# One product for v and U of a head in a chunked RWKV-7 plus SiLU kernel, with a planner that judges by four cases

## The chip, the cores and the metric

The kernel runs on one NeuronCore of a Trainium2 chip. Its engines work side by side from queues of their own: TensorE (PE; its weight loads are listed apart as PEld), VectorE (DVE), ScalarE (ACT), GpSimd (POOL) and SyncE (SP), which here only issues DMAs. The metric is the device time of one execution in microseconds (us), lower is better. The clock of TensorE is granted in steps; the profile gives the share of full speed.

## The reference

The first part is a recurrence over 768 tokens for 4 batches and 8 heads of width 40. The second feeds its output, 3072 tokens of 320 channels, through a feed-forward layer of width 2048.

```python
for t in range(S):
    kt, vt, rt = (k[:, :, t], v[:, :, t], r[:, :, t])
    wt, at, bt = (w[:, :, t], a[:, :, t], b[:, :, t])
    y[:, :, t] = np.einsum('bhd,bhde->bhe', rt, state)
    Sa = np.einsum('bhde,bhe->bhd', state, at)
    state_decay = state * wt[:, :, None, :] - np.einsum('bhd,bhe->bhde', Sa, bt)
    state = state_decay + np.einsum('bhd,bhe->bhde', vt, kt)
...
h = x @ w_in
g = h * (1.0 / (1.0 + np.exp(-h)))
return (g @ w_out)
```

Everything is float32.

## The kernel before

**Steps.** The tokens are cut into 12 steps of C = 64. Within a step the recurrence is written as products of 64 x 64 and 64 x 40 blocks for each of the 32 pairs of batch and head. A step n has these parts, each a function that adds operations to a plan:

- `load` and `load_r` bring a, b, k, w, r and v by DMAs on SP's queue; `prepare` makes decayed copies with scans on DVE and the block products on PE (line 682);
- `special` (steps 0 to 2) and `inverse` with `merge` (later steps) give the inverse X of a triangular block;
- `chain` makes R, then U = -(X R) in two layouts. `solve` (line 1135) gives it by token for the state's update (line 1223). `solve_t` (line 1166) gives it by channel, and the copy `turned` takes it on ACT from PSUM to SBUF (a helper records it as line 407);
- `read` makes the output. In `look` (line 1269) r is multiplied with v and with U, all by channel. DVE masks the result (line 1281) into `lam`; `write` (line 1323) multiplies that with kt, DVE scales it (line 1334), and the result goes by DMA through DRAM to `xt`;
- `moe` is the feed-forward part: `full` (line 1405), `rest` (line 1418), SiLU on ACT (line 1428), `second` (line 1445), a copy on DVE and the output's DMA. Its products are added to the plan for every step and fill PE between the small products of the other parts.

In the first steps `weights` also turns the float64 weights into float32 on DVE and ACT, with some sums on PE (line 508).

**The look products.** Partitions 0 to 39 hold the channels of heads of one group (b = 0), partitions 64 to 103 those of the other. `vut` is a tile of [128, 2, 16, 64]: index 1 is the role, v in half 0 and U in half 1. For each m (half of the heads) `look` issues 32 products: 16 heads, each with v and with U. The weights are 40 partitions by 64 columns of `vut`, the moving operand is 64 columns of r. The result of v goes to the half b of the PSUM partitions, that of U to the other half, in the bank b. In the profile a float32 product is two pairs of a weight load (LDWEIGHTS) and a product (MATMUL), so that a look shows 64 pairs.

v arrives in `vut` by four DMAs a step, each of 48 partitions by 2 x 256 floats. `turned` copies all 128 partitions of the PSUM tile in one instruction (in step 0, halves m go one by one).

**The order.** Nothing is ordered by hand. `Plan.order` simulates the engines: each operation has a cost, keys that it reads and writes, PSUM rooms and a priority, and the next on each engine is the one that can start soonest, with priority as a weighted bonus. On PE it adds a change of shape (`turn`, with LEAVE and ENTER) and the fetch of instructions in blocks of 256 (`walk`). `best` draws 10 settings of the weights and then takes 400 steps of a random search with a fixed seed. Each order found is timed by `through` under several CASES (fetch times, DMA rate, hop between engines, slowness of DVE), and the order with the smallest sum is issued. So a changed cost, key, shape or case can change the order of every engine's instructions.

Of the kernel before, what the change touches and what calls it, by code (L numbers as in the profile page):

```python
# [11 lines left out]
F32 = mybir.dt.float32  # L12
# [21 lines left out]
class Plan:  # L34
# [32 lines left out]
    RATE, LAND = 300.0, 2.0  # L67
    COLD = 42.0
    URGE = {"SP": 0.0, "ACT": 0.03, "PE": 0.05, "DVE": 0.1, "POOL": 0.02}
    LEAVE = {"F": 0.09, "R": 0.2, "T": 0.13, "Q": 0.13, "H": 0.12, "S": 0.11}  # L70
    ENTER = {"F": 0.08, "R": 0.1, "T": 0.03, "Q": 0.03, "H": 0.03, "S": 0.03}

    def turn(self, op):

# [102 lines left out]
    def through(self, out, crowd, rate, hop, slower):  # L177
# [6 lines left out]
        fetched, count, shape, work = [0.0, 0.0], 0, "Q", {}  # L184
        before, after = self.SLOW
        width, few = self.WINDOW, self.FEW
        for op in out:
            e = op["engine"]
            s = at[e]
            for b in op["before"]:  # L190
                s = max(s, end[b] + (hop if self.ops[b]["engine"] != e else 0.0))
            for place in op["takes"]:
                s = max(s, free.get(place, 0.0))
            if e == "PE":
                self.shape = shape
                t, shape = s + self.turn(op), op["shape"]
                to_ = count + op["k"]
                step = op["cost"] / op["k"]
                while count < to_:
                    block = count // 256  # L200
                    gate = 256 * block + 194
                    if len(fetched) == block + 1:
                        full = crowd if max(queue.values()) > t + 1 else 0.0
                        fetched.append(max(t + 0.4, fetched[-1] + before) + after + full)
                    if count >= gate:
                        t = max(t, fetched[-1] + 0.1)
                    to = min(to_, gate if count < gate else 256 * block + 256)
                    left, count = (to - count) * step, to
                    while left > 1e-9:
# [79 lines left out]
def kernel(  # L289
# [15 lines left out]
    nc = tc.nc  # L305
# [5 lines left out]
    T = B * C  # L311
# [65 lines left out]
    def act(n):  # L377
        return 0.19 + n * 0.00082
# [11 lines left out]
    def half(i):  # L390
        return slice(64 * i, 64 * i + 64)
# [193 lines left out]
    def load_r(n):  # L585
        pri = 10 * n - 4
        late = [[("@", ("in", "X", 0))], [("@", ("xt", 0, 0))]][n] if n < 2 else []
        for b in range(2):
            for j in range(2):
                src = most(j)  # L590
                dma(
                    lambda b=b, j=j, src=src: nc.sync.dma_start(
                        rs[most(b), 8 * j : 8 * j + 8].rearrange("p (m q) t -> p m (q t)", m=2), channel(rT, n)[b, src]
                    ),
                    80,
                    late,
                    [("r", b, j)],
                    pri,
                )
                dma(  # L600
                    lambda b=b, j=j, src=src: nc.sync.dma_start(
                        vut[most(b), 0, 8 * j : 8 * j + 8].rearrange("p (m q) t -> p m (q t)", m=2), channel(vT, n)[b, src]
                    ),
                    80,
                    late,
                    [("vt", b, j)],
                    pri,
                )

    def prepare(n):  # L610
        pri = 10 * (n - 2) + 6 if n != 1 else -8
# [480 lines left out]
    def chain(n):  # L1092
# [78 lines left out]
                        stop=True,  # L1171
                    )

        def turned(part, pw):
            c = slice(256 * part[0], 256 * part[-1] + 256)
            copy(
                "ACT",
                vut[:, 1].rearrange("p (g x) t -> p x g t", x=2)[:, :, 4 * part[0] : 4 * part[-1] + 4],
                pw.tile[:, :, c].rearrange("p x (g t) -> p x g t", t=C),
                -1.0,  # L1180
            )

        for part in halves(n):
            l = len(part)
            p_ = pri + 0.2 if n else pri - 0.5
            xp = [k for k in xkeys if k[0] != "X2" or k[2] in part]
            pw = pw_[part]
            add("PE", 0.46 * l, partial(solve_t, part, pw), [*xp, ("R", i3)], [pw, *[("ut", m) for m in part]], p_, [pw], 64 * l)
# [58 lines left out]
    def read(n):  # L1247
# [3 lines left out]
        Z = wz[i3][:, 0 : Q * C]  # L1251
        allw = [("wz", i3)]
        ktk = [("kt", i3, 0), ("kt", i3, 1)]
        rk, vtk = [("r", b, j) for b in range(2) for j in range(2)], [("vt", b, j) for b in range(2) for j in range(2)]
        lam, lks = [], []
        for m in range(2):
            pl, la, lk = Room("pair", 2), Room("lam", 3), []
            lam.append(la)
            if n == 0:
                la.tile, lk = ((at[0], [("a", 0)]), (sbs[0], [("sb", 0)]))[m]  # L1260
                lks += lk
            lr = [la] if n else []

            def look(m=m, pl=pl):
                for o in problems("j", "z", "x", "role", "b"):
                    b, j, x, z, role = (o[k] for k in ("b", "j", "x", "z", "role"))
                    hh, c = 8 * j + 4 * m + 2 * z + x, 4 * j + 2 * z + x
                    hu = 8 * m + 4 * j + 2 * z + x if role else hh
                    nc.tensor.matmul(  # L1269
                        pl.tile[half(1 - b if role else b), b, c * C : c * C + C],  # L1270
                        lhsT=vut[rows(b), role, hu, :],
                        rhs=rs[rows(b), hh, :],
                        start=True,
                        stop=True,
                    )
# [384 lines left out]
```

## Time and profile before

| | |
|---|---|
| median of 3 runs | 736.9 us (732.19, 736.9, 741.88) |
| the profiled execution | 742.53 us, span 740.8 us, 27,279 instructions |
| mean granted clock of PE | 0.976 |
| DVE busy | 419.5 us (57%) |
| ACT busy | 194.6 us (26%) |
| DMA | 77.15 MB, 117,979 packets, mean 104 GB/s |
| half-clock stretches of PE after 40 us, by the clock record | 53.2 to 66.9, 77.1 to 80.5, 200.0 to 203.4, 247.8 to 251.2, 565.2 to 572.0 us, and the end |
| first feed-forward product (line 1405) | 77.24 us |
| U copies on ACT (line 407, vut) | 13, of 1.02 us each (0.60 us for the two halves of step 0) |
| look products (line 1269) | 1,536 pairs, from 58.9 to 666.0 us |

The profile is one execution. A row of instructions gives line, engine, operation, tiles out<-in, shapes, count, busy time and mean length of one, then the idle time of the engine just before them with what ended it. Products overlap in PE's pipeline: the mean of 228 ns for a look product is a latency, and the rate is read from the timeline, where 128 pairs of looks pass in about 2 us.

### The profile page before, as it was taken

What the parts mean: (1) busy time and instruction counts of PE and PEld (TensorE: products, weight loads), DVE (VectorE), ACT (ScalarE), POOL (GpSimd) and SP (SyncE); (2) the same over time, 40 slices, a digit from 0 to 9 for tenths busy, and PEclk for the clock granted to TensorE, in tenths of its full rate; (3) what the DMA queues carried; (4) which work ended last, traced back from release to release, by engine and by line L of the source; (5) the groups of instructions that cost most, each with busy time, mean ns of one, the idle gap of its engine ahead of it and who ended that gap; (6) DMA issues with size and microseconds to landing.
All of it is one profiled execution on the core that took longest, in us unless ns stands there. A gap on an engine that the chain in (4) does not pass through costs nothing.

```text
span 740.8 us, 27279 instructions
## 1 busy us (share of the span) xinstructions
PE 674.7 (91%) x12666; PEld 540.5 (73%) x12666; DVE 419.5 (57%) x614; ACT 194.6 (26%) x241; POOL 14.3 (2%) x31
## 2 busy tenths in 40 slices
PE   2179799898899999999999999899999999999995
PEld 2176577678678677878778878778777778788773
DVE  6845799976479256299273397362686449321000
ACT  3251635523212411404304205124114211202020
POOL 2300000000000000000000000000000000000000
PEclk9996999999999999999999999999998999999998
DMA  7770654742632453525353506333233321401000
GB/s 248 160 227 11 195 210 126 222 116 47 161 107 58 96 135 98 139 61 125 112 133 106 161 19 144 95 99 92 73 93 81 97 60 32 126 21 41 18 1 22
DMA packets 117979, 77.15 MB, mean 104 GB/s; under 512 B 65506, under 2 KB 114338, under 8 KB 117218
## 3 DMA queue, kind: packets, MB, share of 16 engines
q1 hardware_dynamic: 113352, 64.54, 32.9%
q0 software_dynamic: 2096, 10.49, 4.3%
q8 instruction: 101, 1.65, 0.9%
q10 hardware_dynamic: 2410, 0.30, 0.3%
q14 instruction: 20, 0.16, 0.1%
HBM read 60.29 MB, written 14.61 MB: 101 GB/s over the span
## 4 chain that ended last, share of the span: by engine, by line
PE 80%; DVE 8%; DMA 3%; ACT 3%; issue 3%; SPq 1%; ACTq 1%; DVEq 0%
PE pair L1445 27%; PE pair L1405 21%; PE pair L1418 5%; PE pair L1269 4%; PE pair L682 3%; PE pair L1323 3%; PE pair L958 2%; PE pair L1135 2%; PE pair L1223 2%; PE pair L1068 1%; PE pair L1166 1%; PE pair L508 1%; PE pair L744 1%; PE pair L1308 1%; PE pair L1111 1%
## 5 line engine op out<-in xcount | busy, mean ns | idle before, releaser
L1445 PE MATMUL pair<-wo,gts 128*128 128x320 f32 x768 | 219.8, 442 | 1.1 <-issue 1.1
L1445 PEld LDWEIGHTS pair<-wo,gts 128*128 128x128 f32 x768 | 144.7, 192 | 60.4 <-issue 4.3
L1405 PE MATMUL pair<-xt,wi 128*128 128x256 f32 x768 | 175.5, 386 | 1.6 <-ACT R L756 1.3
L1405 PEld LDWEIGHTS pair<-xt,wi 128*128 128x128 f32 x768 | 145.7, 192 | 24.5 <-ACT R L756 1.4
L1428 ACT ACTIVATE gts<-pair 128x1024 f32<-128x1024 f32 x48 | 46.5, 1020 | 134.5 <-PE pair L1418 108.3
L682 PE MATMUL pair<-a,kb 40*64 40x64 f32 x1536 | 32.2, 236 | 35.8 <-DVE a L654 28.7
L1457 DVE COPY ot<-pair 128x320 f32<-128x320 f32 x24 | 11.8, 490 | 92.4 <-PE pair L1445 88.9
L796 DVE TENSOR_REDUCE XI<-XI 128x64 f32<-128x512 f32 (+9 forms) x85 | 58.6, 690 | 2.9
L682 PEld LDWEIGHTS pair<-a,kb 40*64 40x64 f32 x1536 | 28.6, 149 | 38.5 <-issue 20.5
L1418 PE MATMUL pair<-xt,wi 64*128 64x256 f32 x384 | 47.9, 389 | 0.0
L1281 DVE TENSOR_TENSOR lam<-pair,ml 128x1024 f32<-128x1024 f32 x22 | 26.4, 1220 | 32.9 <-PE pair L1269 30.4
L1418 PEld LDWEIGHTS pair<-xt,wi 64*128 64x128 f32 x384 | 35.1, 187 | 6.7 <-issue 2.6
L795 DVE TENSOR_TENSOR XI<-XI,mi 128x1024 f32<-128x1024 f32 (+8 forms) x60 | 33.6, 559 | 9.6 <-DMA mi<-md 8.3
L1334 DVE TENSOR_TENSOR lam<-pair,wz 128x1024 f32<-128x1024 f32 x11 | 13.5, 1223 | 38.8 <-PE pair L1323 38.8
L1269 PEld LDWEIGHTS pair<-r,vut 40*64 40x64 f32 x1536 | 25.9, 142 | 6.8 <-issue 5.9
L664 DVE TENSOR_TENSOR kb<-kbv 128x512 f32<-128x512 f32 (+1 forms) x36 | 29.7, 861 | 0.3
L1269 PE MATMUL pair<-r,vut 40*64 40x64 f32 x1536 | 28.5, 228 | 1.2 <-issue 1.2
L627 DVE TENSOR_TENSOR_SCAN kbv<-wz,zt 128x1024 f32<-128x1024 f32 x12 | 27.5, 2291 | 0.5
L645 DVE TENSOR_TENSOR_SCAN wz<-wz,zt 128x1024 f32<-128x1024 f32 x12 | 27.5, 2289 | 0.3
L756 ACT COPY R<-pair 128x640 f32<-128x640 f32 x12 | 8.3, 693 | 67.1 <-PE pair L744 61.5
L795 DVE TENSOR_TENSOR XI<-XI,xs 128x1024 f32<-128x1024 f32 (+1 forms) x25 | 25.3, 1010 | 0.8
L407 ACT ACTIVATE vu<-pair 64x640 f32<-64x640 f32 x13 | 9.1, 698 | 60.3 <-PE pair L1135 59.4
(151 smaller groups left out, 687.7 us busy)
## 6 DMA issues: line engine op xcount, KB each, us to landing
wz<-in_wT SPq DMA_DIRECT2D x12, 512.0 KB
kbv<-in_bT SPq DMA_DIRECT2D x12, 512.0 KB
a<-in_aT SPq DMA_DIRECT2D x12, 512.0 KB
kbv<-in_kT SPq DMA_DIRECT2D x12, 512.0 KB
r<-in_rT SPq DMA_DIRECT2D x48, 96.0 KB
vut<-in_vT SPq DMA_DIRECT2D x48, 96.0 KB
vu<-in_v SPq DMA_DIRECT2D x24, 160.0 KB
out<-ot SPq DMA_DIRECT2D x48, 80.0 KB
```

The costliest lines, as they stand in the source:

```text
L627: nc.vector.tensor_tensor_scan(back(V), back(W[:, 2 : 2 + Q * C]), zt, 1.0, ALU.mult, ALU.add)
L645: nc.vector.tensor_tensor_scan(Z, Z, zt, 0.0, ALU.mult, ALU.add)
L664: TTn[engine].tensor_tensor(out=at_(kb, place(is_b, first), (576 * step, 4 // step), (128, 4), (1, C)), in0=blocks((kf, bf)[is_b]), in1=bl ...
L682: nc.tensor.matmul(room.tile[half(b), j, g * C : g * C + C], lhsT=kb[rows(j), place(is_b, q) : place(is_b, q) + C], rhs=A[rows(j), q * C : ...
L795: nc.vector.tensor_tensor(out=at_(tmp, 0, *dims), in0=x, in1=y, op=ALU.mult)
L796: nc.vector.tensor_reduce(out=out_, in_=at_(tmp, 0, *dims), axis=AX.X, op=ALU.add)
L1269: nc.tensor.matmul(pl.tile[half(1 - b if role else b), b, c * C : c * C + C], lhsT=vut[rows(b), role, hu, :], rhs=rs[rows(b), hh, :], star ...
L1281: lambda pl=pl, la=la: nc.vector.tensor_tensor(out=la.tile.rearrange("p (q t) -> p q t", q=Q), in0=pl.tile.rearrange("p a b -> p (a b)").r ...
L1405: nc.tensor.matmul(rooms[g].tile[:, f // 2, (f % 2) * T : (f % 2) * T + T], lhsT=wi[:, k, (4 * g + f) * 128 : (4 * g + f) * 128 + 128], rh ...
L1418: nc.tensor.matmul(rooms[g].tile[:, h, (f % 2) * T : (f % 2) * T + T], lhsT=wi3[half(h), g * 256 + (f % 2) * 128 : g * 256 + (f % 2) * 128 ...
L1428: nc.scalar.activation(out=gts[:, 4 * g * T : 4 * g * T + 4 * T], in_=rooms[g].tile.rearrange("p a b -> p (a b)"), func=AF.Silu)
L1445: nc.tensor.matmul(po[b].tile[:, 0, 0:DM], lhsT=g4[:, f, 128 * b : 128 * b + 128], rhs=wo[:, f, :], start=f == 0, stop=f == NF - 1,)
```

## The change

The planner's shapes get a new one, L. Its costs on PE are the same as before but with half the instructions (k from 128 to 64). `vut` becomes [128, 16, 2, 64], so that v and U of a head are neighbours. In group b, v lies in slot b and U in slot 1 - b; so one product with 128 columns of weights writes all 128 PSUM partitions, in the layout that two products gave. v's heads are stored in the order that U's had. Its DMAs are split by m, eight a step, each of 48 partitions by 4 runs of 64 floats, 128 floats apart. `turned` becomes two copies of 40 partitions, one for each b. `look` of half m waits for v of that m alone.

The planner's judgement is changed too: four cases in place of three, each with its own fetch times and crowding; a clock model that counts half-speed work half, and that asks for more work in a window to leave half speed (0.48) than to stay at full speed (0.38).

```diff
-    LEAVE = {"F": 0.09, "R": 0.2, "T": 0.13, "Q": 0.13, "H": 0.12, "S": 0.11}
+    LEAVE = {"F": 0.09, "R": 0.2, "T": 0.13, "Q": 0.13, "H": 0.12, "S": 0.11, "L": 0.13}
...
-    SLOW = 2.8, 1.7
-    CASES = (1.0, 300.0, 0.15, 1.0), (1.5, 240.0, 0.15, 1.0), (1.5, 240.0, 0.25, 1.04)
-    WINDOW, FEW = 3.41, 0.42
+    CASES = (
+        (2.0, 1.9, 3.0, 300.0, 0.35, 1.0),
+        (2.6, 1.3, 1.5, 240.0, 0.25, 1.0),
+        (2.0, 1.9, 1.5, 240.0, 0.25, 1.05),
+        (2.6, 1.9, 0.0, 300.0, 0.25, 1.05),
+    )
+    WINDOW, FEW = 3.41, (0.38, 0.48)
...
-                        pace = 0.5 if t > 30 and work.get(w - 1, 0.0) < few * width else 1.0
+                        if w > window:
+                            known = w == window + 1 and work >= few[pace < 1.0] * width
+                            window, work, pace = w, 0.0, 1.0 if known else 0.5
                         d = min((w + 1) * width - t + 1e-9, left / pace)
-                        work[w] = work.get(w, 0.0) + d
+                        work += d * pace
...
-    vut = sb.tile([128, 2, Q, C], F32, name="vut")
+    vut = sb.tile([128, Q, 2, C], F32, name="vut")
...
-                dma(
-                    lambda b=b, j=j, src=src: nc.sync.dma_start(
-                        vut[most(b), 0, 8 * j : 8 * j + 8].rearrange("p (m q) t -> p m (q t)", m=2), channel(vT, n)[b, src]
-                    ),
-                    80,
+                for m in range(2):
+                    dma(
+                        lambda b=b, j=j, m=m, src=src: nc.sync.dma_start(
+                            vut[most(b), 8 * m + 4 * j : 8 * m + 4 * j + 4, b],
+                            channel(vT, n)[b, src, m].rearrange("p (q t) -> p q t", q=4),
+                        ),
+                        55,
...
-                vut[:, 1].rearrange("p (g x) t -> p x g t", x=2)[:, :, 4 * part[0] : 4 * part[-1] + 4],
-                pw.tile[:, :, c].rearrange("p x (g t) -> p x g t", t=C),
+                vut[rows(b), :, 1 - b].rearrange("p (g x) t -> p x g t", x=2)[:, :, 4 * part[0] : 4 * part[-1] + 4],
+                pw.tile[rows(b), :, c].rearrange("p x (g t) -> p x g t", t=C),
...
-            add("ACT", act(512 * l), partial(turned, part, pw), [pw], [("ut", m) for m in part], p_, [pw])
+            for b in range(2):
+                add("ACT", act(512 * l), partial(turned, part, pw, b), [pw], [("ut", m, b) for m in part], p_, [pw])
...
-                for o in problems("j", "z", "x", "role", "b"):
-                    b, j, x, z, role = (o[k] for k in ("b", "j", "x", "z", "role"))
-                    hh, c = 8 * j + 4 * m + 2 * z + x, 4 * j + 2 * z + x
-                    hu = 8 * m + 4 * j + 2 * z + x if role else hh
+                for o in problems("j", "z", "x", "b"):
+                    b, j, x, z = (o[k] for k in "bjxz")
+                    c = 4 * j + 2 * z + x
+                    hh, hu = 8 * j + 4 * m + 2 * z + x, 8 * m + c
                     nc.tensor.matmul(
-                        pl.tile[half(1 - b if role else b), b, c * C : c * C + C],
-                        lhsT=vut[rows(b), role, hu, :],
+                        pl.tile[:, b, c * C : c * C + C],
+                        lhsT=vut[rows(b), hu].rearrange("p r t -> p (r t)"),
                         rhs=rs[rows(b), hh, :],
...
-            add("PE", 0.9, look, rk + vtk + [("ut", m)], [pl], pri, [pl, *lr], 128)
+            add("PE", 0.9, look, rk + vtk[m] + [("ut", m, b) for b in range(2)], [pl], pri, [pl, *lr], 64, shape="L")
```

The planner issues the whole program in a new order. On PE it stays close to the one before in its large blocks; between them the small products change places, and the weight sums (line 508) that stood between the first looks and the products behind them now follow that first chain.

More of the change, by code (lines that the diff above doesn't have):

```diff
@@ L69 @@
     URGE = {"SP": 0.0, "ACT": 0.03, "PE": 0.05, "DVE": 0.1, "POOL": 0.02}
-    LEAVE = {"F": 0.09, "R": 0.2, "T": 0.13, "Q": 0.13, "H": 0.12, "S": 0.11}
-    ENTER = {"F": 0.08, "R": 0.1, "T": 0.03, "Q": 0.03, "H": 0.03, "S": 0.03}
+    LEAVE = {"F": 0.09, "R": 0.2, "T": 0.13, "Q": 0.13, "H": 0.12, "S": 0.11, "L": 0.13}
+    ENTER = {"F": 0.08, "R": 0.1, "T": 0.03, "Q": 0.03, "H": 0.03, "S": 0.03, "L": 0.03}
     def turn(self, op):
@@ L171, in order, with through @@
         return out
-    SLOW = 2.8, 1.7
-    CASES = (1.0, 300.0, 0.15, 1.0), (1.5, 240.0, 0.15, 1.0), (1.5, 240.0, 0.25, 1.04)
-    WINDOW, FEW = 3.41, 0.42
-    def through(self, out, crowd, rate, hop, slower):
+    CASES = (
[5 more added lines that the diff above has]
+    WINDOW, FEW = 3.41, (0.38, 0.48)
+    def through(self, out, before, after, crowd, rate, hop, slower):
         at = dict.fromkeys(self.HOP, 0.0)
@@ L183, in through @@
         end, free = [0.0] * len(out), {}
-        fetched, count, shape, work = [0.0, 0.0], 0, "Q", {}
-        before, after = self.SLOW
+        fetched, count, shape = [0.0, 0.0], 0, "Q"
+        window, work, pace = -1, 0.0, 0.5
         width, few = self.WINDOW, self.FEW
@@ L599, in load_r @@
                 )
-                dma(
-                    lambda b=b, j=j, src=src: nc.sync.dma_start(
-                        vut[most(b), 0, 8 * j : 8 * j + 8].rearrange("p (m q) t -> p m (q t)", m=2), channel(vT, n)[b, src]
-                    ),
-                    80,
[L605 to L608, printed above, removed]
+                for m in range(2):
[5 more added lines that the diff above has]
+                        55,
+                        late,
+                        [("vt", b, j, m)],
+                        pri,
+                    )
     def prepare(n):
@@ L1172, in solve_t, with turned @@
                     )
-        def turned(part, pw):
+        def turned(part, pw, b):
             c = slice(256 * part[0], 256 * part[-1] + 256)
@@ L1187, in chain @@
             pw = pw_[part]
-            add("PE", 0.46 * l, partial(solve_t, part, pw), [*xp, ("R", i3)], [pw, *[("ut", m) for m in part]], p_, [pw], 64 * l)
-            add("ACT", act(512 * l), partial(turned, part, pw), [pw], [("ut", m) for m in part], p_, [pw])
+            add("PE", 0.46 * l, partial(solve_t, part, pw), [*xp, ("R", i3)], [pw, *[("ut", m, b) for m in part for b in range(2)]], p_, [pw], 64 * l)
+            for b in range(2):
+                add("ACT", act(512 * l), partial(turned, part, pw, b), [pw], [("ut", m, b) for m in part], p_, [pw])
         if n:
@@ L1253, in read @@
         ktk = [("kt", i3, 0), ("kt", i3, 1)]
-        rk, vtk = [("r", b, j) for b in range(2) for j in range(2)], [("vt", b, j) for b in range(2) for j in range(2)]
+        rk, vtk = [("r", b, j) for b in range(2) for j in range(2)], [[("vt", b, j, m) for b in range(2) for j in range(2)] for m in range(2)]
         lam, lks = [], []
```

## Prediction

> **What bounds the kernel now.** I read the page's busy table first, then the list of waits, then single stretches of the timeline, then the shapes table.
>
> ```profile
> PE 674.7 (91%) x12666; PEld 540.5 (73%) x12666; DVE 419.5 (57%) x614; ACT 194.6 (26%) x241; POOL 14.3 (2%) x31
> PE 80%; DVE 8%; DMA 3%; ACT 3%; issue 3%; SPq 1%; ACTq 1%; DVEq 0%
> 140.00:200.00 60.00, 54.76 (x1180) 45.89 (x1180) 41.67 (x66) 16.38 (x22) 1.12 (x2) 1.00 0.51 137
> 200.00:260.00 60.00, 57.78 (x842) 44.20 (x841) 38.72 (x59) 15.39 (x20) 0.00 (x0) 0.94 0.32 85
> 560.00:620.00 60.00, 57.46 (x1288) 46.62 (x1286) 31.67 (x55) 14.21 (x20) 0.00 (x0) 0.94 0.26 63
> ```
>
> TensorE (PE) bounds it: 91% busy, 80% of the chain of waits. The stage lines (span, PE, weight loads, DVE, ACT, POOL, granted clock, DMA share, GB/s) show PE idle 0.3 to 5 us of each 60 us after 140. The feed-forward products fill it: at full clock one pair (a weight load and a product) costs 272 ns on L1445 (17.43 us for 64) and 222 ns on L1405. Pricing every pair of the before order by such rows gives 641 us. So some 100 us of the 740.8 us span are anything else: 13.8 us before the first product, 14.9 us of waiting for the first scans, some 8 us after the last product, half-clock time, other gaps, and pipeline turns. Only the last three can be moved much by this change.
>
> ```profile
> PE pair L682 <- issue: 5.5, 6, 2.8
> PE pair L1223 <- DVE vu L411: 2.1, 3, 0.8
> ...
> 194.36 1.67 PE L682 MATMUL pair<-a,kb 40*64 40x64 f32 x97
> 198.79 0.69 PE L682 MATMUL pair<-a,kb 40*64 40x64 f32 x31 [2.77 <-issue]
> ...
> 470.31 2.02 PE L1269 MATMUL pair<-r,vut 40*64 40x64 f32 x121
> 472.79 0.34 PE L1269 MATMUL pair<-r,vut 40*64 40x64 f32 x7 [0.47 <-issue]
> ```
>
> "Issue" waits cut a uniform group in its middle, with no data to wait for. The cuts near 464.5, 468.2 and 472.8 are exactly 128 pairs apart (x63+x64+x1, then x7+x121): 256 instructions. PE waits there for its program. These waits sum to 14.1 us (5.5+3.2+1.2+1.1+1.0+0.9+0.5+0.4+0.3), 10.3 of them after 140 us. The 2.77 us one is followed by the clock at 0.62 from 199 to 203.
>
> ```profile
> L1269 PE MATMUL pair<-r,vut 40*64 40x64 f32 x1536 | 28.5, 228 | 1.2 <-issue 1.2
> L1323 PE MATMUL pair<-lam,kt 128*40 128x64 f32 x704 | 22.1, 220 | 0.3 <-issue 0.3
> L769 PE MATMUL pair<-ident,kb 40*128 40x40 f32 x384 | 17.0, 246 | 1.6 <-ACT ZQ L405 0.9 <-DVE vu L411 0.8
> L407 ACT ACTIVATE vut<-pair 128x1024 f32<-128x1024 f32 x11 | 11.3, 1024 | 13.3 <-PE pair L1166 13.1 <-ACT GT L1209 0.2
> ```
>
> These price the change: today's look products, two shapes near the new one, and the copy that is split.
>
> **What the Trainium skill says.** "Runtime: NRT & Kernel Launch", Instruction fetch mechanics: instructions come in 16 KiB blocks of 256, and the fetch is mostly hidden. The block agrees (101 instruction packets of 16 KB on the page, cuts every 256); "hidden" does not, 14.1 us show. "TensorE: Matmul & The Clock Gate", Part 1: the clock is halved after a window of about 3.4 us with little PE work; the trace has half clock in stretches of 3.4 us or multiples. Its section LDWEIGHTS has load time rise with the number of columns, P/1.2 ns: 107 ns for 128 columns. The L769 row speaks against it as a throughput: 32 such pairs pass in 1.07 us, 33 ns each. "DMA: Bandwidth & Descriptors", Why small descriptors are slow: below 512 B a fixed cost counts. In the trace's packet records the mean is 12.6 ns at 128 B and 55 ns at 1024 B.
>
> **The change, part by part.**
>
> 1. *Look products.* Per look, 64 pairs in four quadrants become 32 pairs of 128 columns in two row halves; 24 looks, so 768 pairs go (12,666 to 11,898). Today a look takes 1.01 us (2.02 us for 128 pairs): 15.8 ns a pair. New pair, upper side: L769 with equal weights, 33 ns. Lower side: L1323, also two tiles of 64 moving columns, 1.92 us for 64, 30 ns. At 32 pairs that is 0.96 to 1.06 us: I take the dear one, 24 x 0.05 = **+1 us** (bounds -1 and, with loads that overlap badly, +17: the rival D2 below). So the array itself gains nothing.
>
> 2. *Program fetch.* 1,536 instructions fewer are 6 blocks of 99. In array time, blocks of 128 pairs that last under 3 us number 21 in the order before and 17 in the order after, placed from the same offset. In proportion 14.1 us become 11.4. Three of the stalls before (2.77, 0.75 and 0.47 us) lie in or just behind blocks that held 50 to 120 look pairs, which now last twice as long per pair. I take **-4 us** (bounds -10, +3[...]).
>
> 3. *The order.* The planner now judges by four cases, with a clock model that counts half-speed work half and asks more work to leave the half clock. So the whole order of all engines is new. On PE, the stretch of weight sums (L508) that stood between the first looks and their use moves behind the first chain, and the solve-to-update distance grows: before, five of eleven solves had only 0.98 to 1.43 us of PE work between them and the update (the 2.1 us and 0.8 us waits for DVE's vu come from there); after, three have, while five have 3.2 us or more. Waits for data on PE after 140 us sum to about 8 us (2.1+1.3+0.9+0.8+0.7+0.6 and smaller), between 40 and 140 us to about 8 more. I take **-3 us** (bounds -8, +8; what is late next is the U copy, item 5).
>
> 4. *Clock.* Lost to half clock: 60 us at 0.94 twice, 7.2 us; 24 us at 0.86 and 20 us at 0.76 in the start (36 to 80), 8.2 us; together 15.4. Fewer stalls of the 2.8 us kind leave fewer poor windows. I take a little under half, **-7 us** (bounds -13, +6: the new order has stretches of small products of its own).
>
> 5. *U copies.* Each of the 12 steps copies U per head group, 40 partitions instead of 128, but as many elements: two of 1.02 us for one. ACT +12 us, at 26% busy. The look waits for both, 1.02 us later, and everything behind it in PE's queue with it. After solve_t, the new order puts 3.5 to 9.5 us of PE work ahead of the look in ten of twelve steps, against some 2.2 us that the two copies need; it is 2.4 us in step 9 and 1.1 to 1.6 us in step 0, which runs at half clock. Cost **0** in the sum, +2 at most from steps 0 and 9; if that cover were gone, 12 x 1.02 = 12 us.
>
> 6. *v loads.* 48 DMAs become 96 of half the size, runs of 1 KB become 256 B. Interpolating between the two packet rows gives 18.7 ns: per step 1,536 packets x 18.7 / 16 engines = 1.8 us against 384 x 55 / 16 = 1.3. SP issues 48 more at a median 0.43 us, 1.7 us per step, and what stands behind (the next step's token-wise v, md, xh) starts so much later. SP waits over 400 us in its own list, and v is wanted some 40 us after its issue: **0**. In the start, where DMA is 0.7 busy, it puts the second step's ms store back 1.7 us; that chain had slack (its products waited for weights work on DVE until 87): 0, at most +2.
>
> Sum: +1 - 4 - 3 - 7 = **-13 us**. The profiled execution took 742.5 us (span 740.8 and 1.7 around it), so 729.5 for its like; it lies 5.6 above the median of the runs, 736.9, from which I predict **724 us**. Within 2% means 722.2 to 751.6; that is about what a measurement of this kernel can tell from no change.
>
> **The rivals.**
>
> *B, an exchange (737 us).* Stalls and poor windows are moved, not removed: 17 short blocks are still there, and each is a chance for a 2.8 us stall with 1.7 us of half clock behind it. For it: the three runs before already spread by 9.7 us with one order.
>
> *C, nearly all of it goes (713 us).* No poor window after 140 (-7), three quarters of the start's (-6), fetch at a third (-9), waits -3, looks +1: -24. For it: each cause feeds the next, as at 198.8. Against: 17 short blocks.
>
> *D, slower (753 us).* The start falls to half clock and stays. Place: 40 to 85 us, where the new order runs solve, looks, update, write and the next step's products with no weight sums between. Those fillers kept PE 8 of 8 us busy from 58 to 66. Price: half clock throughout 40 to 85 in place of 53 to 67 and 77 to 80.5 is 28 us more of it, 14 us lost, with 2 us for the copies of step 0. It decides once the first chain leaves PE under about half busy in each window. Against: DVE, not PE, limits 80 to 140 (28.8 of 30 us busy from 110), so part would be absorbed. *D2*, of the same size: 128-column loads at 107 ns over two tiles, 53 ns a pair, 1.71 us a look, 24 x 0.70 = +17 us; decides above some 50 ns a pair, and L769's 33 ns speaks against it.
>
> That the looks don't merge isn't possible: the new program holds 16 look products where 32 stood.
>
> **How the numbers follow.** The main case 0.58 (own range 713 to 735, 45% of it below 722.2), B 0.13, C 0.16, D with D2 0.13. Faster: 0.26 + 0.16 = 0.42. Slower: 0.12 of D. Same: 0.46. Range 708 to 748: outside lie most of D and the best of C.
>
> **What would show it.** L1269's successor with 768 pairs and about 1.0 us a look (above 1.2: D2); issue waits on PE near 10 us; clock of the span above 0.985 (now 0.976); vut copies 24 of 1.02 us with no PE wait for them but in steps 0 and 9. A start whose first feed-forward product comes later than 77.2 us, or a clock below 0.7 beyond 67 us, would show me wrong towards D; issue waits still at 14 us towards B.

## The result and the profile after

The changed kernel takes 767.19 us (median of 6 runs, 765.43 to 771.38); the kernel before, run beside it, takes 740.24 us (6 runs, 732.19 to 743.76). The ratio is 1.0394, with a 95% interval of 1.035 to 1.0437: slower, where 724 us was predicted. Ratios here and below are taken over the undisturbed runs of both kernels, so they need not be the quotient of the medians. The profiled execution after took 767.32 us, its span is 765.5 us, and PE's mean clock is 0.965.

The page of the changed kernel: the busy table, the chain of waits by engine, the groups of the looks and of the U copies, and the instruction queue.

```profile
PE 699.1 (91%) x11898; PEld 567.5 (74%) x11898; DVE 419.5 (55%) x614; ACT 207.1 (27%) x254; POOL 14.5 (2%) x31
PE 78%; DVE 10%; issue 5%; DMA 3%; SPq 2%; ACT 1%; ACTq 0%; DVEq 0%
L1279 PEld LDWEIGHTS pair<-r,vut 40*128 40x128 f32 x768 | 45.5, 190 | 3.2 <-issue 2.7
L1279 PE MATMUL pair<-r,vut 40*128 40x64 f32 x768 | 47.0, 275 | 0.9 <-issue 0.9
L414 ACT ACTIVATE vut<-pair 40x1024 f32<-40x1024 f32 (+1 forms) x26 | 24.8, 953 | 26.5 <-PE pair L1175 25.9
q8 instruction: 95, 1.56, 0.9%
```

PE has 768 pairs fewer and is busy 24.4 us longer (699.1 against 674.7). Three quarters of that stand in one row: the looks, which were 1,536 pairs in 28.5 us of busy time, are 768 pairs in 47.0 us. A look takes 1.96 us (47.0 / 24) where 1.0 was forecast. The instruction packets fell as forecast, from 101 to 95.

The list of PE's waits of the changed kernel (line waiting, releaser, total, times, longest):

```profile
PE pair L691 <- issue: 15.9, 3, 14.1
PE pair L691 <- DVE a L663: 14.0, 2, 13.8
PE pair L1318 <- DMA r<-in_rT: 6.8, 3, 4.1
PE pair L1077 <- DMA X<-xd: 3.2, 1, 3.2
PE pair L922 <- issue: 2.8, 1, 2.8
```

The first two rows together are the waits for the first scans; the 14.1 us is no program fetch, for the kernel before shows the same gap of the start under DVE (14.9 us). Without it the fetch waits sum to 10.3 us. The third row is new in this size: products with the state (line 1318) wait for r, and so for DMAs on SP's queue.

The stage lines of the changed kernel (span, PE, weight loads, DVE, ACT, POOL, granted clock, DMA share, GB/s):

```profile
140.00:200.00 60.00, 55.76 (x1004) 46.38 (x998) 44.27 (x70) 20.95 (x26) 1.11 (x2) 0.97 0.40 110
200.00:260.00 60.00, 55.60 (x912) 44.68 (x914) 40.27 (x60) 15.19 (x19) 0.00 (x0) 0.93 0.41 101
560.00:620.00 60.00, 58.13 (x1208) 47.09 (x1207) 36.33 (x53) 17.02 (x21) 0.00 (x0) 0.94 0.33 78
```

The clock didn't rise: 0.97, 0.93 and 0.94 stand where 1.00, 0.94 and 0.94 stood. By the clock record the half-clock time after the first full-clock moment is 53.0 us against 35.6. The ledger of the two profiled executions:

| term, us | before | after | difference |
|---|---|---|---|
| look products, busy | 28.5 | 47.0 | +18.5 |
| PE waits for its program | 14.1 | 10.3 | -3.8 |
| PE waits for data | 15.7 | 20.0 | +4.3 |
| half clock, counted half | 17.8 | 26.5 | +8.7 |
| sum | | | +27.7 |
| span | 740.8 | 765.5 | +24.7 |

The ledger is not a full account: waits and looks at half clock count in two rows, and the busy time of other products isn't in it. Why the sum lies 3 us above the span's difference is not resolved.

### The profile page after: what moved, and what is told of

It reads as the page before. It is cut to its first block, busy times and chain, and to the rows that moved or that the text cites. A ratio compares the mean times of both kernels' runs of the same rounds, so it can differ in the third digit from the quotient of the medians.

```text
span 765.5 us, 25839 instructions
## 1 busy us (share of the span) xinstructions
PE 699.1 (91%) x11898; PEld 567.5 (74%) x11898; DVE 419.5 (55%) x614; ACT 207.1 (27%) x254; POOL 14.5 (2%) x31
## 4 chain that ended last, share of the span: by engine, by line
PE 78%; DVE 10%; issue 5%; DMA 3%; SPq 2%; ACT 1%; ACTq 0%; DVEq 0%
PE pair L1455 25%; PE pair L1415 20%; PE pair L1279 6%; PE pair L1428 5%; PE pair L1333 3%; PE pair L967 3%; PE pair L691 3%; PE pair L1233 2%; PE pair L1175 2%; PE pair L1144 2%; DVE XI L804 2%; DVE XI L805 1%; PE pair L778 1%; PE pair L1318 1%; PE pair L1077 1%
## 5 line engine op out<-in xcount | busy, mean ns | idle before, releaser
L1467 DVE COPY ot<-pair 128x320 f32<-128x320 f32 x24 | 11.7, 488 | 79.9 <-PE pair L1455 77.8
L1279 PEld LDWEIGHTS pair<-r,vut 40*128 40x128 f32 x768 | 45.5, 190 | 3.2 <-issue 2.7
L1279 PE MATMUL pair<-r,vut 40*128 40x64 f32 x768 | 47.0, 275 | 0.9 <-issue 0.9
L1010 ACT COPY mi<-XI 128x1024 f32<-128x1024 f32 x5 | 10.1, 2019 | 80.9 <-DVE XI L805 80.9
L414 ACT ACTIVATE vut<-pair 40x1024 f32<-40x1024 f32 (+1 forms) x26 | 24.8, 953 | 26.5 <-PE pair L1175 25.9
L791 ACT COPY kt<-pair 128x640 f32<-128x640 f32 x24 | 16.0, 694 | 37.1 <-PE pair L778 20.5
```

The costliest lines, as they stand in the source:

```text
L1279: nc.tensor.matmul(pl.tile[:, b, c * C : c * C + C], lhsT=vut[rows(b), hu].rearrange("p r t -> p (r t)"), rhs=rs[rows(b), hh, :], start=Tr ...
```

## Experiments

### What the wide product costs

The first question is whether the wide look itself costs time, or the order and the layout that came with it. Two pairs of kernels that differ in the look alone answer it. `merge_old_order` keeps the planner and the order of the kernel before and takes the new layout, the split loads, the two copies and the wide look. Its edit, against the kernel before:

```diff
-    vut = sb.tile([128, 2, Q, C], F32, name="vut")
+    vut = sb.tile([128, Q, 2, C], F32, name="vut")
...
+                    for m in range(2):
+                        nc.sync.dma_start(
+                            vut[most(b), 8 * m + 4 * j : 8 * m + 4 * j + 4, b],
+                            channel(vT, n)[b, src, m].rearrange("p (q t) -> p q t", q=4),
...
-                        pl.tile[half(1 - b if role else b), b, c * C : c * C + C],
-                        lhsT=vut[rows(b), role, hu, :],
+                        pl.tile[:, b, c * C : c * C + C],
+                        lhsT=vut[rows(b), hu].rearrange("p r t -> p (r t)"),
```

> The merged look with its layout, its two copies and its split loads, but with the planner's costs, shapes and cases of before: the instructions of every engine stand in the order of before, except that each look has 32 pairs for 64. Theory W (the wide product is the loss): a look takes 1.96 us instead of 1.19 as in the changed kernel, +18 us, less about 3 us of program fetch: 752 to 759 us. Rival O (the new order is the loss, and the looks' longer busy time is only time in which PE would have waited): within 5 us of before, 735 to 745.

Measured: 782.95 us (4 runs), ratio 1.0583 (1.0492 to 1.0673): on the side of theory W, but 24 us above its range.

`quads_new_layout` is that kernel with the look made of 64-column products again, read from the new layout:

```diff
-                        pl.tile[:, b, c * C : c * C + C],
-                        lhsT=vut[rows(b), hu].rearrange("p r t -> p (r t)"),
+                        pl.tile[half(slot), b, c * C : c * C + C],
+                        lhsT=vut[rows(b), hu, slot, :],
```

> The new layout of v and U, two copies and split loads, in the order of before, but the look stays at 64 pairs in four quadrants. Theory W: the layout costs nothing, 736 to 744 us. Rival L (the second copy and the 256-byte runs delay looks and start): 745 us or more.

Measured: 755.14 us (4 runs), ratio 1.0181 (1.009 to 1.0272): what rival L expected, so the layout isn't free. With the order of the kernel before, the wide look costs 27.8 us. Of that the looks' own busy time is 22.2 us (52.1 against 29.9), and half-clock time rises from 57 to 80 us, 11.6 when counted half (looks that fell into half clock are in both figures); waits for data fall by 5 (23.6 against 28.7). Waits for the program hardly differ (9.5 against 9.0 us), so fewer instructions bought nothing here.

`quads_new_order` makes the same edit in the changed kernel, whose order is kept.

> The changed kernel with its order of every engine, only that each look is issued as 64 pairs in four quadrants. Theory W: the looks give back 18 us and the fetch takes 2 to 4 again: 750 to 753 us, of which some 10 above before are the order's. Rival O: it stays above 760 us.

Measured: 757.99 us (4 runs), ratio 1.0245 (1.0158 to 1.0333), against 1.0394 (1.035 to 1.0437) with the wide look; it lies between the two expectations. The wide look costs 9 to 11 us in its own order (by the medians, or by the ratios): 18 us of busy time (47.0 against 29.0), of which the waits for the program give back 6 (10.3 against 16.2), those for data 3 (20.0 against 23.3) and half clock 2.5 (53.0 against 58.1, counted half); the two profiled spans differ by 7.0. The gain in half clock belongs to this pair of executions: the profiled execution of `quads_new_order` has the lowest clock of its four, and over all runs the wide looks don't have less half clock (item 4 below). It is slower in both orders, and in both the intervals of the ratios with and without it don't meet.

Why is it slow? The timelines of two looks in a row, first of the changed kernel (with what follows), then of `quads_new_order` (start, duration, line, count):

```profile
304.52 3.79 PE L1279 MATMUL pair<-r,vut 40*128 40x64 f32 x64
308.14 1.95 PE L1428 MATMUL pair<-xt,wi 64*128 64x256 f32 x16
309.93 0.64 PE L778 MATMUL pair<-ident,kb 40*128 40x40 f32 x16
```

```profile
305.88 2.10 PE L1280 MATMUL pair<-r,vut 40*64 40x64 f32 x128
```

64 wide pairs hold the array for 3.62 us (304.52 to 308.14), 56.6 ns each; 128 pairs of 64 columns need 2.10 us. The start times of single records show the pattern: wide pairs start 7 ns and then 105 ns apart, the pairs in quadrants 6, 7, 7 and then 38 ns. So a group of tiles that share no rows and columns starts within 7 to 20 ns, and the next group follows 112 ns later with 128 columns of weights, 58 ns with 64. In the wide form a group holds two tiles, in the other four: 56 and 14.6 ns a pair.

Two kernels tell which size sets the 112 ns. `wide_n32` is `merge_old_order` with half as many columns moving, so that half of the look's result is left out:

```diff
-                        pl.tile[:, b, c * C : c * C + C],
+                        pl.tile[:, b, c * C : c * C + C // 2],
...
-                        rhs=rs[rows(b), hh, :],
+                        rhs=rs[rows(b), hh, 0 : C // 2],
```

> merge_old_order, but each wide product moves only 32 of the 64 columns of r, so half of the look's result is left out. A wide pair took 61 ns at full clock. Theory LD (the load of 128 columns sets the pace): still 58 to 62 ns a pair. Rival ST (the two row halves do not overlap, and the 64 moving columns at 0.87 ns set it): 28 to 35 ns.

`wide_c96` is `merge_old_order` with 96 of the 128 columns of weights; a quarter of the look's result is left out:

```diff
-                        pl.tile[:, b, c * C : c * C + C],
-                        lhsT=vut[rows(b), hu].rearrange("p r t -> p (r t)"),
+                        pl.tile[0:96, b, c * C : c * C + C],
+                        lhsT=vut[rows(b), hu].rearrange("p r t -> p (r t)")[:, 0:96],
```

> merge_old_order, but each wide product has 96 of the 128 columns of weights, so a quarter of the look's result is left out. Theory LD (pace by the columns loaded, 53 ns for 128, and 3 more): 42 to 46 ns a pair. Rival (a fixed cost of a pair in a row half, whatever the columns): 54 to 58 ns.

The look's row in the shapes tables and one look in the timelines, of `merge_old_order`, `wide_n32` and `wide_c96` in this order:

```profile
L1269 PE MATMUL pair<-r,vut 40*128 40x64 f32 x768 | 52.1, 294 | 0.0
303.44 2.20 PE L1269 MATMUL pair<-r,vut 40*128 40x64 f32 x32
```

```profile
L1269 PE MATMUL pair<-r,vut 40*128 40x32 f32 x768 | 51.4, 289 | 4.6 <-DVE lam L728 4.6
301.99 2.17 PE L1269 MATMUL pair<-r,vut 40*128 40x32 f32 x32
```

```profile
L1269 PE MATMUL pair<-r,vut 40*96 40x64 f32 x768 | 39.9, 259 | 4.6 <-DVE lam L728 4.6
298.11 1.77 PE L1269 MATMUL pair<-r,vut 40*96 40x64 f32 x32
```

Half the moving columns leave the look as long as it was (2.17 and 2.20 us); three quarters of the weight columns make it some three quarters as long (39.9 / 52.1 = 0.77; 1.77 against 2.20 us for the look shown), and by the start times the groups follow each other after 85 instead of 112 ns. So the columns of weights set the pace of the wide look, and the moving columns don't. (One run each: 785.24 and 763.27 us.) "TensorE: Matmul & The Clock Gate", LDWEIGHTS, in the Trainium skill puts a load at P/1.2 ns for P columns: 107, 80 and 53 ns for 128, 96 and 64. The groups' 112, 85 and 58 ns are that and 5 ns, whether two or four tiles are in the group. The skill's "TensorEngine Tiling (Array Packing)", Key Properties, says that different tiles can load and multiply in parallel, and these looks show what is lost when tiles are widened: four narrow tiles take in 256 columns of weights in 58 ns, two wide ones the same 256 in 112. That it is the load, and not other work that grows with the columns of weights, is read from the fit to this rule; no run separates the two.

The rule has two limits, which the kernel before shows. Its ordinary products on 64 or fewer columns (in the shapes, columns of weights follow the `*`, moving columns the `x`):

```profile
L1223 PE MATMUL pair<-vu,kt 128*40 128x40 f32 x704 | 16.4, 208 | 2.7 <-DVE vu L411 2.1 <-issue 0.5
L1166 PE MATMUL pair<-X,R 64*40 64x64 f32 x768 | 15.3, 229 | 4.8 <-issue 3.2 <-ACT gts L1428 1.6
L1135 PE MATMUL pair<-R,X 64*64 64x40 f32 x704 | 13.4, 235 | 0.4 <-DVE X L409 0.4
```

By the start times of single records at full clock, their groups follow each other after 38 ns (40 columns of weights, 40 moving), 56 ns (40 and 64) and 58 ns (64 and 40). So in these products the larger of the two counts sets the pace; in the narrow look they are equal, and the change doubled the columns of weights alone. The other limit is line 769, transposes with 128 columns of weights: their groups of two follow after 62 ns, not 112. Why is not shown.

### What the v loads and the U copies cost

In the order of the kernel before, without a wide look, the layout with its loads still cost 1.8% (`quads_new_layout`). The next kernels keep that order and make one part each. `two_copies`: the U copy split by b, in the layout of before.

```diff
+            for b in range(2):
...
-                    vut[:, 1].rearrange("p (g x) t -> p x g t", x=2)[:, :, 4 * part[0] : 4 * part[-1] + 4],
-                    pw.tile[:, :, c].rearrange("p x (g t) -> p x g t", t=C),
+                    vut[rows(b), 1].rearrange("p (g x) t -> p x g t", x=2)[:, :, 4 * part[0] : 4 * part[-1] + 4],
+                    pw.tile[rows(b), :, c].rearrange("p x (g t) -> p x g t", t=C),
```

> The kernel of before, order kept, with U copied by two instructions of 40 partitions for one of 128. quads_new_layout lost 16 us against before with the order kept. Theory V (the v loads are the loss: in that trace the first r and v loads hold SP's queue from 35.0 to 47.1 us for 34.3 to 38.8, and r comes late at 86.8 and 149.7): this one costs 0 to 3 us, 738 to 743. Rival U (the second copy delays looks and what stands behind them): 748 us or more.

Measured: ratio 1.0038 (0.9993 to 1.0084), medians 746.42 (20 runs) and 740.75 us (39 runs). Inconclusive, and between the two expectations: anything from nothing to 0.8%. (The medians, over all runs, lie 0.8% apart.)

`eight_loads`: the v loads split by m, still in runs of 1 KB.

```diff
-                        vut[most(b), 0, 8 * j : 8 * j + 8].rearrange("p (m q) t -> p m (q t)", m=2), channel(vT, n)[b, src]
+                    for m in range(2):
+                            vut[most(b), 0, 8 * j + 4 * m : 8 * j + 4 * m + 4].rearrange("p q t -> p (q t)"),
+                            channel(vT, n)[b, src, m],
```

> The kernel of before, order kept, with each v load split in two by m; runs stay at 1 KB. Theory V1 (the number of loads counts): 744 to 752 us. Theory V2 (their 256-byte runs count, since each issue took 0.6 us in place of 0.43 and the queue stalled behind them): 738 to 743 us.

Measured: 745.74 us (20 runs), ratio 1.0059 (1.0031 to 1.0088), in the range of theory V1: the number of loads counts.

`runs_256`: as `eight_loads`, with v and U of a head side by side, so that the runs are 256 bytes; one U copy, narrow looks.

```diff
-    vut = sb.tile([128, 2, Q, C], F32, name="vut")
+    vut = sb.tile([128, Q, 2, C], F32, name="vut")
...
-                            vut[most(b), 0, 8 * j + 4 * m : 8 * j + 4 * m + 4].rearrange("p q t -> p (q t)"),
-                            channel(vT, n)[b, src, m],
+                            vut[most(b), 8 * j + 4 * m : 8 * j + 4 * m + 4, 0],
+                            channel(vT, n)[b, src, m].rearrange("p (q t) -> p q t", q=4),
```

> As eight_loads, but v and U interleaved, so that v lands in 256-byte runs; U by one copy of 128 partitions; looks in quadrants; order kept. Theory V in all: 749 to 757 us, near quads_new_layout. Rival U: 738 to 745 us. The distance to eight_loads is the price of the short runs.

Measured: 756.18 us (4 runs), ratio 1.0217 (1.0128 to 1.0306), on the same chip and beside the same runs as `eight_loads`. By the medians the short runs cost some 10 us more, but that size is uncertain: the four runs are two near 752 and two near 760 us, and the profiled executions of the two kernels lie only 3.7 us apart (752.49 and 748.74, the latter near the top of its 20 runs). Most of the loss against the kernel before arises early: the products of line 1166 that stand at 111.8 us there come 6.6 us later, those at 181.4 us 9.3 us later; between 220 and 360 us the distance is 6.5 to 7.5, at the end 9.9. SP's timelines of the start show what changes there, first of `eight_loads`, then of `runs_256`:

```profile
39.65 2.57 SPq L602 DMA_DIRECT2D vut<-in_vT  x2
42.83 1.53 SPq L575 DMA_DIRECT2D vu<-in_v  x2
46.44 6.59 SPq L698 DMA_DIRECT2D ms<-sb  x8
56.16 0.34 SPq L870 DMA_DIRECT2D xs<-ms  x1
```

```profile
41.71 3.00 SPq L602 DMA_DIRECT2D vut<-in_vT  x2
46.67 5.21 SPq L575 DMA_DIRECT2D vu<-in_v  x2
51.99 5.44 SPq L698 DMA_DIRECT2D ms<-sb  x8
60.33 0.34 SPq L870 DMA_DIRECT2D xs<-ms  x1
```

Two issues of v span 3.00 us, and the two of `vu` behind them 5.21 us instead of 1.53. By the single records each issue still lasts 0.56 to 0.63 us; it is the next one that starts only 2.45 and 4.59 us after it. SP's queue stands. The store `xs`, the last of these, is issued at 60.33 us; in the kernel before it was 53.60. The stage line of the kernel before shows what is special about this time: the DMA engines are full (share 1.07, 330 GB/s). There too SP stood, but in the stores behind the loads (eight issues of `ms` in 11.96 us). That full engines hold the queue is read from this coincidence, and it isn't the whole of it: in `runs_256` the share is 1.07 to 1.09 from 40 to 48 us, but 0.64 from 48 to 52, where the queue still stands. No run sets it apart from, for one, the number of packets that are waiting.

```profile
40.00:44.00 4.00, 4.00 (x112) 3.81 (x106) 0.28 (x1) 3.73 (x7) 0.00 (x0) 1.00 1.07 330
```

If SP's queue alone were the trouble, another queue would free it. `runs_256_act` moves the v loads of steps 0 and 1 to ACT's queue, and `before_act` does so in the kernel before:

```diff
-                        nc.sync.dma_start(
+                        (nc.scalar if n < 2 else nc.sync).dma_start(
```

> runs_256, order kept, with the v loads of steps 0 and 1 issued on ACT's queue in place of SP's. Theory Q (the short runs cost by blocking SP's queue, behind which r, the token-wise v and the ms stores of the start stand): 738 to 746 us. Rival D (their time on the DMA engines themselves): it stays at 752 to 758 us.

> The kernel of before with the v loads of steps 0 and 1 on ACT's queue, all else kept. Theory Q gives a gain here too, where r is late by 1 to 2 us: 733 to 740 us. Rival: SP was not late before, and ACT loses what it issues: 739 to 746 us.

Measured: 750.7 us (4 runs), ratio 1.0173 (1.0121 to 1.0225), and 737.69 us (4 runs), ratio 0.9998 (0.9944 to 1.0051), no gain. The first met neither expectation: its interval overlaps that of `runs_256`, and its trace shows the hold-up on another engine. ACT's timeline in `runs_256_act` (in brackets the idle time before the instruction, and its releaser):

```profile
37.19 1.55 ACTq L602 DMA_DIRECT2D vut<-in_vT  x2
47.78 4.96 ACTq L602 DMA_DIRECT2D vut<-in_vT  x2
52.78 1.07 ACT L405 COPY XI<-pair 128x512 f32<-128x512 f32 x2 [10.19 <-DMA vut<-in_vT]
```

Now ACT stands in its issues, 4.96 us for two, and the copy behind them comes 10.19 us late; PE then waits 11.7 us for it. The skill's "DMA: Bandwidth & Descriptors", Issuing engines are not separate DMA queues, says that DMAs of all issuing engines run on the same 16 engines. The hold-up that moved along to ACT agrees with that; but here too the second issue ends at 52.74 us, when the engines' share is down to 0.51 (48 to 52 us). Where loads have long runs, the queue makes no difference (`before_act`).

`quads_long_runs` asks the same in the changed order: it is `quads_new_order` with v and U kept apart, and thus runs of 1 KB.

```diff
-    vut = sb.tile([128, Q, 2, C], F32, name="vut")
+    vut = sb.tile([128, 2, Q, C], F32, name="vut")
...
-                            vut[most(b), 8 * m + 4 * j : 8 * m + 4 * j + 4, b],
-                            channel(vT, n)[b, src, m].rearrange("p (q t) -> p q t", q=4),
+                            vut[most(b), 0, 8 * m + 4 * j : 8 * m + 4 * j + 4].rearrange("p q t -> p (q t)"),
+                            channel(vT, n)[b, src, m],
```

> quads_new_order with v and U kept apart, so that the eight v loads of a step have runs of 1 KB again; order, two copies and look products as there. Theory V2 (short runs hold the start back in the new order too): 744 to 751 us, 7 to 14 below quads_new_order's 758. Rival: the new order has room for them, 755 to 760 us.

Measured: 750.71 us (4 runs), ratio 1.0164 (1.0115 to 1.0213), 7 us below `quads_new_order`, as theory V2 expected, though the two intervals overlap. In its trace the last product of the looks starts at 675.0 us, against 686.8, and 693.7 in the changed kernel; the waits for r are 3.7 us, against 5.6 and 6.8.

How r is held up in the changed kernel is seen at the next step's loads. SP's timeline, then PE's:

```profile
74.33 0.60 SPq L599 DMA_DIRECT2D r<-in_rT  x1
74.98 1.30 SPq L609 DMA_DIRECT2D vut<-in_vT  x2
...
81.38 0.53 SPq L599 DMA_DIRECT2D r<-in_rT  x1
82.36 1.31 SPq L609 DMA_DIRECT2D vut<-in_vT  x2
```

```profile
77.36 0.27 PE L1318 MATMUL pair<-r,GT 40*40 40x64 f32 x2 [1.13 <-DMA r<-in_rT]
81.73 0.44 PE L1318 MATMUL pair<-r,GT 40*40 40x64 f32 x4 [4.11 <-DMA r<-in_rT]
83.71 1.93 PE L1318 MATMUL pair<-r,GT 40*40 40x64 f32 x58 [1.53 <-DMA r<-in_rT]
85.56 4.88 PE L1415 MATMUL pair<-xt,wi 128*128 128x256 f32 x16
```

The DMA engines aren't full here (share 0.31 and 0.35 in the two stretches of 4 us from 74 us on); it is the issues that are longer. The four loads of r alternate with pairs of v loads of 1.2 to 1.3 us, so that the last of them is issued 7.05 us after the first (81.38 - 74.33); in the kernel before it was 3.51 (79.29 - 75.78, with issues of 0.4 us). PE gets r in three parts with 6.8 us of waiting, and the first feed-forward product comes at 85.56 us instead of 77.24. It comes at 80.38 in `quads_long_runs` and at 83.29 in `quads_new_order`.

The order has a share in this. In the kernel before the same products stand behind the first 16 feed-forward products and wait for nothing:

```profile
82.50 1.10 PE L1308 MATMUL pair<-r,GT 40*40 40x64 f32 x64
```

The new order puts them ahead, where even the long runs of `quads_long_runs` leave 3.7 us of waiting for r.

### What the judgement by four cases costs

`four_cases` is the kernel before with only the planner's cases and clock model changed, as in the diff of the change; its computation and operations are those of before, in another order.

```diff
-    CASES = (1.0, 300.0, 0.15, 1.0), (1.5, 240.0, 0.15, 1.0), (1.5, 240.0, 0.25, 1.04)
-    WINDOW, FEW = 3.41, 0.42
+    CASES = (
+        (2.0, 1.9, 3.0, 300.0, 0.35, 1.0),
+        (2.6, 1.3, 1.5, 240.0, 0.25, 1.0),
...
+    WINDOW, FEW = 3.41, (0.38, 0.48)
```

> The kernel of before with nothing changed but the planner's four cases and its clock model, so an order of its own. If judging by four cases makes worse orders by itself (theory W puts about 8 us of the loss on order and clock), 745 to 752 us; if the new order is bad only because of the wider looks and split loads that it had to place, 732 to 742 us.

Measured: 744.38 us (19 runs), ratio 1.0066 (1.0036 to 1.0097). A little slower, just under the first of the two expected ranges. In its profiled execution (740.02 us, the low end of its runs) data waits fell to 9.7 us and half clock to 27.6, while waits for the program rose from 14.1 to 20.5 us; that execution is no slower than the one of the kernel before, so it doesn't show where the 0.66% lies.

### The sum

| kernel, in the changed order | ratio | what it adds |
|---|---|---|
| `quads_long_runs` | 1.0164 | the order, eight v loads a step, two U copies |
| `quads_new_order` | 1.0245 | runs of 256 bytes, +0.8% |
| the changed kernel | 1.0394 | the wide looks, +1.5% |

Taken alone in or from the kernel before, four cases (0.66%), eight loads (0.59%) and two copies (0.38%, not clear of none) add up to 1.63%, which fits the first row; since an order is drawn anew for each set of costs, that is no proof of it. No kernel tried was faster than the kernel before.

## Why the prediction was wrong, point by point

Forecast (-13 us) and ledger (+27.7) are 41 us apart: 17.5 in the looks, 15.7 in the clock, 7.3 in the waits for data.

**Item 1, look products: the step that failed first.** It took +1 us by the rows of L769 (33 ns a pair) and L1323 (30 ns); measured is +18.5. The rival D2 had the right mechanism and nearly the right size: it said 53 ns a pair, 1.71 us a look and +17 us, against 56, 1.96 and +18.5 (the 1.96 us contain the latency of a look's last pair, 0.27 us). It was set aside because L769 has 128 columns of weights at 33 ns. But L769 is a transpose (the code has `is_transpose=True`), and the page of before shows that it isn't an ordinary product: 32 of them a step give 384 pairs in 12 steps, one each, where the look's products show two. So the upper neighbour was of another kind, and the lower one, L1323, loads 40 columns of weights, not 128. The runs with 96 columns and with 32 moving columns show that the pace goes with the columns of weights.

**Item 2, program fetch: right in number, in part by luck.** -4 us forecast, -3.8 measured, packets 101 to 95. In the changed order, narrow looks wait 16.2 us for the program (21.4 in `quads_long_runs`) and wide looks 10.3: the new order makes these waits longer, and the wide looks then take back more than was forecast. In the old order there was no such gain (9.0 and 9.5), so it is a gain of that order with those looks, not of the count alone. The traces in the old order with narrow looks differ among themselves by more than 3.8 us (9.0 in `quads_new_layout`, 14.6 in `before_act`).

**Item 3, the order: wrong in sign.** -3 us forecast; the four cases alone cost 0.66%, about 5 us, and waits for data rose by 4.3. The waits named in the prediction did shrink, but r and X by DMA came late instead. The plan also counts a wide look at 0.9 us, as it did a narrow one (the last line of the change's diff), where the chip takes 1.96, so the new order was drawn for looks of half their length; no run with the true cost was made. The order is still the better one for wide looks: `merge_old_order` has them in the old one and takes 16 us more (782.95 against 767.19).

**Item 4, clock: wrong in sign.** -7 us forecast, +8.7 measured (half of 17.4 us). The start (up to 88 us) has 17 us of half clock in both kernels. The new poor windows come later, above all 13.7 us from 255.2 on where the kernel before has 3.4. `quads_long_runs` has such a stretch of 13.7 us near 250 and `quads_new_order` one of 17.1, so it belongs to the new order. How much of the sum the wide looks bring can't be read from single traces: in the old order half clock is 57 us without them and 80 with them, in the new one 58 and 53. The median clock of all runs says more: 0.979 for the kernel before (22 runs), 0.972 for `quads_long_runs`, 0.966 for `quads_new_order` (4 each), 0.963 for the changed kernel (6). With the spans that is, as an estimate, 31, 42, 51 and 57 us of half clock, so in the new order most of the rise was there before the looks were widened.

**Item 5, U copies: right, as far as it could be resolved.** The page has 26 copies, 24.8 us in all, and PE waited for one twice, 0.6 and 0.2 us. Alone they cost between nothing and 0.8%.

**Item 6, v loads: wrong.** 0 was forecast, with +2 at most for the start. The packets were priced rightly: 18.5 ns at 256 bytes, where 18.7 was interpolated. What was missed is that a DMA issue isn't a fixed 0.43 us. With 256-byte runs it takes 0.59, so eight hold SP 3.0 us a step longer than four did, not 1.7; and at and just after the time of full DMA engines issues stood 2.2 to 4.6 us apart, so that the queue behind them, `xs` in it, waited. r in the next step is late through the longer issues, not through full engines. The split costs 0.59%, and in the old order the short runs bring it to 2.2%. The prediction read the DMA share in the start as 0.7, a mean over 24 us (36 to 60) that hides 12 us at 0.95 to 1.07.

**Rival D** named the place, 40 to 85 us, but another mechanism (too little PE work). The first feed-forward product did come 8.3 us later and half clock did last to 87.9 us, but in the sum the start has no more of it than before, and r's late loads, with the order that puts their products first, stand directly ahead of the late product.

## What to carry to other kernels

Price a changed product by its own kind: before a row is taken as a neighbour, count its pairs per product, and where weights are reloaded for every product, ask how many tiles load at once and with how many columns, since fewer instructions with wider weights can hold the array longer. Before a DMA is split or its runs are shortened, look at the DMA share in windows of a few us where it is issued, and at what stands behind it in its queue. A new order drawn by a planner is a part of the change with a cost of its own; run it alone.

## What the runs showed of the hardware that was not expected

- In ordinary float32 products that reload their weights each time, the larger of two counts set the pace of a group: 38 ns with 40 columns of weights and 40 moving, 56 with 40 and 64, 58 with 64 and 40, 112 with 128 and 64. Transposes with 128 columns of weights took 62 ns a group.
- Halving the moving columns from 64 to 32 left a wide look unchanged (2.20 and 2.17 us); a group of disjoint tiles followed the last after 58, 85 and 112 ns with 64, 96 and 128 columns of weights, with four, two and two tiles in it.
- A load of 48 KB in 256-byte runs took 0.59 us to issue in the median, where 1 KB runs took 0.43 for 96 KB and 0.42 for 48 KB (`eight_loads`); at and just after a time of full DMA engines (share 1.03 to 1.09), two issues in short runs held SP for 3.00 us and ACT for 4.96.
